# Attention and experts on one core: the first three pairs' steps reordered, a masked low operand, constant rows by one copy

## The chip, the cores and the metric

The kernel runs on one core of a Trainium2 chip. The metric is the device time of one execution in microseconds (us), lower is better. TensorE is called PE, VectorE DVE, ScalarE ACT, GpSimd POOL and SyncE SP, as in the profile.

## What is computed

The reference is attention with pooled queries, and then a mixture of experts on its output.

```python
def _attn_ref(q, k, v):                       # 8 batches, 8 heads, 1152 keys, head size 64
    q_pool = q.reshape(B, H, S // 2, 2, D).mean(axis=3)
    scores = scale * np.matmul(q_pool, k.transpose(0, 1, 3, 2))
    scores = scores - np.max(scores, axis=-1, keepdims=True)
    attn = np.exp(scores)
    attn = attn / (np.sum(attn, axis=-1, keepdims=True) + 1e-09)
    return np.matmul(attn, v)
# moe on x = attn_out as (4608, 512): 8 experts, hidden size 1024
e_idx = np.argmax(x @ w_gate, axis=1)
gate_w = softmax(x @ w_gate)[arange, e_idx];  eom = 1 / (1 + np.exp(-(x @ w_output_gate)))
out[mask] = gate_w[mask, None] * eom[mask, e, None] * (np.maximum(x[mask] @ w1[e], 0) @ w2[e])
```

## The kernel before, in words

The attention part works on 32 pairs of heads (8 batches, 4 pairs each), one after the other, and the expert part follows. To keep float32 accuracy with float16 matmuls, every operand is kept as a high part and a low part, the rest that the high part leaves.

For each pair, `prep` holds a set of small steps. The keys (`kpf`) and the summed queries (`qs`) are scaled by a power of two that comes from the magnitude of the keys (`kabs` on ACT, a matmul `gk`, three tiny DVE steps `ksc`), then split into high parts (`xk`, `xq`) and low parts (`kp`, `yq`). From these come the operands of the matmuls: `ka` (high keys, twice), `kb` (low keys in rows 0 to 63 and constant rows 64 to 68), `qa` (high and low queries), `qb` (high queries and rows for the row maxima), and `qd` (a block of high queries for the low keys of the mixed tile, in which 64 queries of the first head and 64 of the second share a tile). Pairs 3 and later get these operands by DMA copies. The first pair gets them by matmuls with selection matrices (`sk` for the high keys, `sl` for the low keys, `sq0` and `sq1` for the queries, each by key half or head) and casts out of PSUM. The second pair gets its high keys that way and the rest by DMA. The values are split in the same manner (`amax`, `gmax`, `scale`, `vh`, `vs`, `vl`).

Then three generators run, interleaved by hand:

- `mgen` makes the row maxima. A pair has 9 query tiles with 3 key chunks each, so 27 maxima: two matmuls (three for the mixed tile) into one of three PSUM banks, and one DVE reduction (line 397). After a group of 5 and a group of 4 tiles the maxima are combined (line 404), turned by a PE transpose (line 431), split in two pieces `mr` (lines 435 and 436) and sent into `qb` by two DMAs in ACT's queue (line 146).
- `sgen` makes the scores (line 474), 18 a pair, each 128 keys by 512 queries in two matmuls; the second one, with `qb`, takes the maximum off, so the first score waits for the DMAs of the first group. ACT takes the exponential (line 450). The low part of the result is made by POOL (line 458), or for some scores by DVE (line 455) from a second exponential that ACT writes (line 452). The scores have four PSUM banks.
- `agen` multiplies with the values (lines 503 to 505), six scores behind.

The order on PE, DVE, ACT and POOL is what the program writes. The main loop makes one score per step `s` and asks `prep_at` three times a step (one "row" each) for the steps of the tables that are due: `PREPF` for the first pair, `PREP0` for the second, `PREPE` for the third, `PREP` for the others. A table entry is a row number and a step. `L0` says how many steps before the first score the maxima begin, and `LS` by how much that lead grows per step. `WARM` says how many dummy matmuls on a constant (`idle`, line 129) stand at some places; the first number is that of the dummies at the program's very start.

At the start, DVE fills rows of `qb`, POOL builds the identity, the constants and the selection matrices, and three POOL fills (line 199) write the constant rows 64 to 68 of the first `kb`, 2304 columns of float16 each: first all five rows, then four, then three over them. Copies of these rows go to the other two `kb` by DMA.

Of the kernel before, what the change touches and what calls it, by code (L numbers as in the profile page):

```python
# [17 lines left out]
PSUM = bass.MemoryType.PSUM  # L18

LEAD = 18  # L20
L0 = 15
LS = 0.2
RI = 7
PREP0 = ((0, 'lk'), (6, 'qsum'), (8, 'kabs'), (11, 'gk'), (12, 'ksc', 0), (12, 'ksc', 1), (13, 'ksc', 2), (14, 'ks', 0), (15, 'kh', 0), (15, 'qs'), (16, 'ks', 1), (17, 'kh', 1), (18, 'qh'), (18, 'kl'), (19, 'ql'), (19, 'dq', 0), (20, 'dq', 1), (22, 'qd'), (23, 'sk', 0, 0), (26, 'sk', 0, 1), (29, 'sk', 1, 0), (32, 'sk', 1, 1), (28, 'dkl', 0), (28, 'dql', 0), (29, 'dkl', 1), (29, 'dql', 1),
        (53, 'lv'), (71, 'amax', 0), (74, 'amax', 1), (81, 'gmax'), (82, 'scale', 0), (85, 'scale', 1), (90, 'scale', 2), (93, 'vh', 0), (93, 'vs', 0), (96, 'vh', 1), (97, 'vl', 0), (100, 'vs', 1), (104, 'vl', 1))
PREPF = ((0, 'lf'), (1, 'fsel'), (2, 'qsv', 0), (3, 'kabs'), (3, 'gk'), (3, 'ksc', 0), (3, 'ksc', 1), (3, 'ksc', 2), (4, 'qsv', 1), (4, 'khs', 0), (5, 'khs', 1), (6, 'klh', 0), (7, 'klh', 1), (8, 'sk', 0, 0), (9, 'sq0'), (10, 'sk', 0, 1), (11, 'sl', 0, 0), (13, 'qd'),
         (45, 'sl', 0, 1), (46, 'sk', 1, 0), (48, 'sk', 1, 1), (51, 'sq1'), (54, 'sl', 1, 0), (57, 'sl', 1, 1), (56, 'lv'),
         (78, 'amax', 0), (82, 'amax', 1), (99, 'gmax'), (100, 'scale', 0), (100, 'scale', 1), (100, 'scale', 2), (103, 'vh', 0), (103, 'vs', 0), (106, 'vh', 1), (107, 'vl', 0), (109, 'vs', 1), (113, 'vl', 1))
FWD = 15
# [45 lines left out]
def attention(tc, qT, kT, vL, wg, keep, xs, cum, pairs, setup, scat, init, exps, moe):  # L75
    nc = tc.nc
    nb = len(pairs) // 4
    with ExitStack() as ctx:
# [1391 lines left out]
```

## Time and profile before

| | us |
|---|---|
| runs | 1398.0, 1397.2, 1404.05 (median 1398.0) |
| profiled execution | 1396.84 |
| its span | 1395.1 |
| PE busy in the span | 1350.2 (97%) |
| DVE busy | 1104.5 (79%) |
| ACT busy | 1033.2 (74%) |
| POOL busy | 968.9 (69%) |
| mean granted PE clock | 0.989 of full |

The span runs from the first to the last instruction of the profiled execution; its own time is 1.74 us longer. Busy time is that of executing instructions. A row of the timeline has the start, the duration, the engine and line, the operation, output and inputs with their shapes, the count of merged instructions, and in brackets the idle time of the engine before it and what ended it. The granted clock is 1.00 at 2.4 GHz and 0.50 at 1.2 GHz.

### The profile page before, as it was taken

How to read it: one execution, taken by the hardware profiler on the slowest of the kernel's cores; microseconds unless marked ns; L12 is line 12 of the kernel's file. 1: busy time of each engine (PE TensorE's matmuls, PEld its weight loads, DVE VectorE, ACT ScalarE, POOL GpSimd, SP SyncE). 2: the span in 40 equal slices, each digit the busy share in tenths (PEclk: the TensorE clock that was granted, in tenths of full speed). 3: DMA queues.
4: the chain of work that ended last, by engine and by line, in shares of the span. 5: the costliest groups of instructions: out<-in, count | busy, mean ns of one | idle time of the engine just before them, and what ended most of it. 6: DMA issues, size and time to landing. Idle time of an engine off the chain costs nothing.

```text
span 1395.1 us, 41903 instructions
## 1 busy us (share of the span) xinstructions
PE 1350.2 (97%) x16827; PEld 935.0 (67%) x16827; DVE 1104.5 (79%) x2615; ACT 1033.2 (74%) x1858; POOL 968.9 (69%) x998
## 2 busy tenths in 40 slices
PE   7899999999999999999999999989999999999998
PEld 4566666766767676766676666666666767767665
DVE  6677886788788888888788788857988787887883
ACT  6788887888988888888888777684557556475672
POOL 6888998999989999999999899874122221322321
PEclk8999999999999999999999999999999999999999
DMA  5345664556547655655565434167876766547762
GB/s 191 105 137 154 179 184 140 155 172 186 168 141 213 175 154 174 179 179 161 169 181 172 126 94 131 50 243 286 309 266 216 271 228 239 198 154 269 269 242 76
DMA packets 103291, 255.76 MB, mean 183 GB/s; under 512 B 13661, under 2 KB 25565, under 8 KB 103087
## 3 DMA queue, kind: packets, MB, share of 16 engines
q1 hardware_dynamic: 92014, 222.55, 50.5%
q0 software_dynamic: 9632, 29.71, 5.9%
q8 instruction: 133, 2.18, 0.7%
q10 hardware_dynamic: 1440, 0.74, 0.2%
q14 instruction: 72, 0.58, 0.1%
HBM read 197.47 MB, written 20.75 MB: 156 GB/s over the span
## 4 chain that ended last, share of the span: by engine, by line
PE 82%; DVE 6%; ACT 4%; DMA 3%; issue 2%; POOL 2%; SPq 0%; ACTq 0%; POOLq 0%; DVEq 0%
PE mp L396 17%; PE sps L474 16%; PE hps L1111 13%; PE av L504 5%; PE av L503 4%; PE av L505 4%; PE yp L1157 4%; PE yp L1156 4%; PE yp L1155 4%; PE sps L484 2%; PE av L514 2%; PE yp L1153 1%; DMA xs<-xb,posi 1%; PE tp L589 1%; PE xps L1092 1%
## 5 line engine op out<-in xcount | busy, mean ns | idle before, releaser
L397 DVE TENSOR_REDUCE pm<-mp 128x1 f32<-128x384 f32 x864 | 449.6, 551 | 109.6 <-PE mp L396 89.7
L458 POOL TENSOR_TENSOR pl<-p 128x512 f16<-128x512 f32 x414 | 425.2, 1044 | 54.0 <-ACT p L450 50.3
L450 ACT ACTIVATE p<-sps 128x512 f32<-128x512 f32 x576 | 340.2, 599 | 123.6 <-PE sps L474 76.8
L396 PE MATMUL mp<-ka,qa 128*128 128x384 f16 x840 | 269.0, 327 | 5.3 <-DVE xl L579 1.7
L505 PE MATMUL av<-vt,pl 128*128 128x65 f16 x2304 | 253.1, 193 | 3.3 <-POOL pl L458 3.1
L503 PE MATMUL av<-vt,p 128*128 128x65 f16 x2304 | 254.0, 193 | 1.4 <-DVE xb L524 1.3
L504 PE MATMUL av<-vt,p 128*128 128x64 f16 x2304 | 253.4, 194 | 0.0
L396 PE MATMUL mp<-kb,qb 66*128 66x384 f16 x768 | 251.6, 328 | 0.0
L503 PEld LDWEIGHTS <-p 128*128 128x128 bf16 x2304 | 215.6, 97 | 32.6 <-DVE xb L524 3.1
L504 PEld LDWEIGHTS <-p 128*128 128x128 bf16 x2304 | 213.8, 98 | 28.5 <-issue 0.2
L474 PE MATMUL sps<-qa,ka 128*128 128x512 f16 x576 | 219.7, 381 | 3.5 <-DVE pl L455 2.4
L474 PE MATMUL sps<-qb,kb 69*128 69x512 f16 x576 | 220.1, 382 | 0.9 <-DMA qb<-mr 0.9
L505 PEld LDWEIGHTS <-pl 128*128 128x128 f16 x2304 | 212.9, 98 | 3.8 <-POOL pl L458 3.4
L1111 PE MATMUL hps<-x,w1h 128*128 128x256 f16 (+2 forms) x1408 | 208.0, 261 | 3.4 <-DVE x L1095 2.0
L1111 PE MATMUL hps<-x,w1l 128*128 128x256 f16 (+2 forms) x704 | 179.1, 261 | 0.0
L1162 POOL DMA_INDIRECT out_dram<-y,ids x35 | 42.4, 1211 | 150.8 <-DVE ids L958 51.5
L1111 PEld LDWEIGHTS <-w1h 128*128 128x128 f16 x1408 | 132.1, 98 | 18.9 <-issue 3.3
L396 PEld LDWEIGHTS <-qa 128*128 128x128 f16 x840 | 82.8, 99 | 74.6 <-issue 4.4
L455 DVE TENSOR_TENSOR pl<-sps,p 128x512 f16<-128x512 f32 x162 | 111.1, 686 | 22.2 <-ACT sps L452 19.4
L396 PEld LDWEIGHTS <-qb 66*128 66x128 f16 x768 | 75.3, 98 | 69.9 <-issue 8.1
L860 POOL DMA_INDIRECT xg<-xs,riD x28 | 39.4, 1408 | 103.8 <-ACT x L1094 77.3
L1157 PE MATMUL yp<-w2h,hl 128*128 128x512 f16 x272 | 103.2, 379 | 4.8 <-DVE hl L1126 4.5
(337 smaller groups left out, 3117.7 us busy)
## 6 DMA issues: line engine op xcount, KB each, us to landing
wst<-in_w_dram SPq DMA_DIRECT2D x64, 512.0 KB
raw1b<-in_w_dram SPq DMA_DIRECT2D x24, 1024.0 KB
raw2b<-in_w_dram SPq DMA_DIRECT2D x24, 1024.0 KB
raw1a<-in_w_dram SPq DMA_DIRECT2D x22, 1024.0 KB
raw2a<-in_w_dram SPq DMA_DIRECT2D x22, 1024.0 KB
vp<-in_vL_dram SPq DMA_DIRECT2D x32, 576.0 KB
kpf<-in_kT_dram SPq DMA_DIRECT2D x31, 576.0 KB
qp<-in_qT_dram SPq DMA_DIRECT2D x31, 576.0 KB
```

Source lines behind the costliest of these rows:

```text
L396: nc.tensor.matmul(mp, lhsT=l, rhs=r, start=j == 0, stop=j == len(ops) - 1)
L397: nc.vector.tensor_reduce(out=pm[:, k:k + 1], in_=mp, axis=AX.X, op=ALU.max)
L450: e_ = nc.scalar.activation(out=p32, in_=x, func=AF.Exp, scale=1.0 / 16)
L455: nc.vector.tensor_tensor(out=pl, in0=x, in1=ph, op=ALU.subtract)
L458: nc.gpsimd.tensor_tensor(out=pl, in0=p32, in1=ph, op=ALU.subtract)
L474: nc.tensor.matmul(x, lhsT=l, rhs=r, start=j == 0, stop=j == 1)
L503: nc.tensor.matmul(av_[:, qb, 0:65], lhsT=hi, rhs=vt[:, h, c, 0:65], start=c == 0 and qb == 0, stop=False)
L504: nc.tensor.matmul(av_[:, qb, 0:64], lhsT=hi, rhs=vt[:, h, c, 66:130], start=False, stop=False)
L505: nc.tensor.matmul(av_[:, qb, 0:65], lhsT=lo, rhs=vt[:, h, c, 0:65], start=False, stop=e and qb == 3 and h == 0)
L1111: nc.tensor.matmul(hp[:, f, 0:v], lhsT=W1[l][g][:, c, fs], rhs=d['x'][:, c, o:o + v], start=f + c + i == 0, stop=f + c + i == 6)
L1155: nc.tensor.matmul(yp, lhsT=d['hh'][:, c, z], rhs=W2[0][:, c], start=c == 0, stop=False)
L1157: nc.tensor.matmul(yp, lhsT=d['hl'][:, c, z], rhs=W2[0][:, c], start=False, stop=c == 7)
```

## The change

The change has these parts.

1. The tables of the first three pairs get other row numbers. In the first pair (`PREPF`), the selections of the first head's first key half come first; those of the second half (`sk 0 1`, `sl 0 1`), of the second head and the second half of the low keys move behind. In the second pair (`PREP0`) the selections and the query steps come later, and all value steps but the load (`lv`) 9 to 12 rows later. In the third pair (`PREPE`) `qs`, `qh`, `dq`, `ql` and `qd` come 6 to 7 rows later, and the DMA copies of the low parts are reordered.
2. `L0` goes from 15 to 13: the maxima begin two steps closer to the first score.
3. The first pair's groups are 4 and 5 tiles instead of 5 and 4, and in the first group the maxima go by key chunk: all four tiles of the first chunk first.
4. `WARM` has 64 instead of 48 dummies at the start, and 22 more behind the first pair's `gk`.
5. The constant rows of `kb` are written to a small tile `kc` of two columns, and one POOL copy spreads it over the 2304 columns, as 1152 float32 words.
6. `qd` is written in full by a POOL scaling with a mask (`hm`, one column per head) in place of two copies of 64 by 64, and needs no fill at the start.

```diff
-L0 = 15
+L0 = 13
...
-PREP0 = ((0, 'lk'), (6, 'qsum'), (8, 'kabs'), (11, 'gk'), ...
+PREP0 = ((0, 'lk'), (6, 'qsum'), (17, 'kabs'), (25, 'gk'), ...
...
-WARM = (48, 30, 32, 0, 12)
+WARM = (64, 30, 32, 0, 12, 22)
...
-        for i in range(2):
-            nc.gpsimd.memset(QDs[i], 0.0)
+        hm = keep['hm']
...
+                kc = sm.tile([KROW, 2], F16, name="kc", bufs=1)
                 for o, w in ((KROW, 16.0 * SHIFT), (68, -1.0), (67, -MLT)):
-                    nc.gpsimd.memset(KBs[0][64:o], w)
+                    nc.gpsimd.memset(kc[64:o], w)
+                nc.gpsimd.tensor_copy(out=KBs[0].bitcast(F32)[64:KROW].rearrange("p h n -> p (h n)"), in_=kc.bitcast(F32)[64:KROW].broadcast_to([KROW - 64, S]))
...
                 nc.tensor.matmul(g[:, 0:1], lhsT=blk, rhs=ak.bitcast(BF16)[:, 1:2], start=True, stop=True)
+                if not n:
+                    idle(ps_a.tile([128, 512], F32, name="idle5", tag="av"), WARM[5])
...
                 for h in range(2):
-                    z = slice(64 * h, 64 * h + 64)
-                    nc.gpsimd.tensor_copy(out=QDs[n % 2][z, z], in_=xq[z, 512 if h == 0 else 0:][:, 0:64])
+                    nc.gpsimd.tensor_scalar(out=QDs[n % 2][:, 64 * h:64 * h + 64], in0=xq[:, 512 if h == 0 else 0:][:, 0:64], scalar1=hm[:, h:h + 1], scalar2=1.0, op0=ALU.mult, op1=ALU.mult)
...
-                for t0, t1 in ((0, 5), (5, 9)):
+                for t0, t1 in ((0, 5), (5, 9)) if n else ((0, 4), (4, 9)):
...
+                    if n == 0 and t0 == 0:
+                        ch.sort(key=lambda x: x[1])
```

DVE, from the first pair's xq to its first reductions. `kp` are the low keys (first half and second half one step each), `sh` is the PSUM output of a selection matmul, `mp` that of a maximum. Before:

```order
L206 TENSOR_SCALAR xq<-qs,ik 128x576
L207 SCALAR_TENSOR_TENSOR yq<-qs,ik,xq 128x576
L215 SCALAR_TENSOR_TENSOR kp_218<-kpf,ik,xk_222 128x576 x2
L270 CAST qa_138<-sh 128x288 x2
L254 CAST kb_132<-sh 64x288 x2
L397 TENSOR_REDUCE pm<-mp_348 128x1
```

The same place on DVE with the change:

```order
L207 TENSOR_SCALAR xq<-qs,ik 128x576
L208 SCALAR_TENSOR_TENSOR yq<-qs,ik,xq 128x576
L216 SCALAR_TENSOR_TENSOR kp_236<-kpf,ik,xk_240 128x576
L273 CAST qa_142<-sh 128x288 x2
L257 CAST kb_136<-sh 64x288 x2
L216 SCALAR_TENSOR_TENSOR kp_236<-kpf,ik,xk_240 128x576
L401 TENSOR_REDUCE pm<-mp_359 128x1
```

The second half of the low keys has moved from ahead of the casts to behind them.

ACT, from the second pair's first scaling to the first exponential. `ka_136` and `ka_140` are the second pair's high keys. With the change (before, the order was that of the steps `qs`, `xq`, the casts mixed with the two sums over `vp`, and then the two DMAs):

```order
L240 ACTIVATE kpf<-kpf,ik 128x576
L286 CAST xk_334<-kpf 128x576
L240 ACTIVATE kpf<-kpf,ik 128x576
L286 CAST xk_334<-kpf 128x576
L257 CAST ka_140<-sh 128x288 x4
L145 DMA qb_145<-mr 1x4x128 x2
L257 CAST ka_140<-sh 128x288 x4
L243 ACTIVATE qs<-qs,ik 128x576
L295 CAST xq<-qs 128x576
L324 ACTIVATE junk,am<-vp 128x576 x2
L454 ACTIVATE p_572<-sps 128x512
```

The DMAs of the row pieces stand ahead of the second four casts, the query steps and the sums.

ACT, from the tenth score of the first pair on: the third pair's steps (`kpf`, `xk`, `qs`, `xq`) and the second pair's sums over `vp` among the exponentials (`p`, `sps`, `pt`). Before:

```order
L450 ACTIVATE p_755<-sps 128x512
L452 ACTIVATE sps<-sps 128x512
L322 ACTIVATE junk,am<-vp 128x576
L283 CAST xk_511<-kpf 128x576
L240 ACTIVATE qs<-qs,ik 128x576
L450 ACTIVATE p_779<-sps 128x512
L452 ACTIVATE sps<-sps 128x512
L450 ACTIVATE pt<-sps 128x384
L322 ACTIVATE junk,am<-vp 128x576
L292 CAST xq<-qs 128x576
L450 ACTIVATE p_835<-sps 128x512
L452 ACTIVATE sps<-sps 128x512
```

The same place on ACT with the change:

```order
L454 ACTIVATE p_786<-sps 128x512
L456 ACTIVATE sps<-sps 128x512
L286 CAST xk_540<-kpf 128x576
L454 ACTIVATE p_806<-sps 128x512
L456 ACTIVATE sps<-sps 128x512
L454 ACTIVATE pt<-sps 128x384
L454 ACTIVATE p_853<-sps 128x512
L456 ACTIVATE sps<-sps 128x512
L454 ACTIVATE pt<-sps 128x384
L243 ACTIVATE qs<-qs,ik 128x576
L454 ACTIVATE p_894<-sps 128x512
L295 CAST xq<-qs 128x576
```

Both sums, `qs` and `xq` have moved behind the exponentials of the eleventh and twelfth scores.

## Rows read from the trace of the kernel before

**Rows 1.** Busy time by stretch: stretch, length, each engine's busy us, clock, DMA.
```profile
0.00:31.00 31.00, 21.09 (x131) 12.71 (x131) 20.42 (x44) 19.46 (x46) 19.82 (x56) 0.83 0.64 209
...
47.40:60.00 12.60, 9.27 (x81) 5.49 (x78) 7.26 (x19) 6.99 (x15) 7.22 (x9) 0.73 0.60 147
...
230.00:500.00 270.00, 268.99 (x4077) 187.44 (x4078) 219.06 (x572) 231.76 (x455) 256.64 (x264) 1.00 0.57 167
```

**Rows 2.** Timeline of the start: start, duration, engine, line, operation, count.
```profile
1.13 4.09 PE L129 MATMUL idle<-ones 128*128 128x128 bf16 x48 [1.13 <-DVE ones L809]
...
4.95 0.81 POOL L196 CAST sel<-ident 128x64 f16<-128x64 f32 x1
...
5.81 6.35 POOL L199 MEMSET kb<- 5x2304 f16 x3
...
8.25 1.96 DVE L206 TENSOR_SCALAR xq<-qs,ik 128x576 f16<-128x576 f32 x1
...
10.24 0.82 DVE L207 SCALAR_TENSOR_TENSOR yq<-qs,ik,xq 128x576 f16<-128x576 f32 x1
...
10.98 1.54 DVE L215 SCALAR_TENSOR_TENSOR kp<-kpf,ik,xk 128x576 f16<-128x576 f32 x2
...
13.17 0.80 DVE L254 CAST kb<-sh 64x288 f16<-64x288 f32 x2
...
15.20 1.39 POOL L289 TENSOR_TENSOR qs<-qp 128x576 f32<-128x576 f32 x1
...
17.32 3.12 DVE L397 TENSOR_REDUCE pm<-mp 128x1 f32<-128x384 f32 x6 [3.35 <-PE mp L396]
```

**Rows 3.** The same timeline, ACT from 15 us to the second pair's first scaling.
```profile
15.05 1.28 ACT L254 CAST ka<-sh 128x288 f16<-128x288 f32 x4
...
19.06 1.17 ACT L219 ACTIVATE kjunk<-kpf 128x1152 f16<-128x1152 f32 x1
...
21.22 0.77 ACT L237 ACTIVATE kpf<-kpf,ik 128x576 f32<-128x576 f32 x1 [0.90 <-DVE ik L233]
```

**Rows 4.** Hand-over to the scores: timelines of DVE and PE, and one chain row.
```profile
26.80 0.17 DVE L404 TENSOR_REDUCE m<-pm 128x5 f32<-128x15 f32 x1
...
27.65 0.27 DVE L436 SCALAR_TENSOR_TENSOR mr<-mr,tp 5x128 f16<-5x128 f16 x1
...
31.06 0.39 PE L474 MATMUL sps<-qb,kb 69*128 69x512 f16 x1 [0.91 <-DMA qb<-mr]
...
31.45 0.66 PE mp L396 x4
```

**Rows 5.** Busy time by stretch, two single microseconds; the clock is third from last.
```profile
7.00:8.00 1.00, 0.16 (x1) 0.10 (x1) 0.19 (x2) 0.52 (x2) 0.94 (x2) 0.59 0.85 217
...
51.00:52.00 1.00, 0.00 (x0) 0.00 (x0) 1.00 (x2) 0.83 (x2) 0.57 (x1) 0.78 0.51 124
```

**Rows 6.** Timelines of ACT, DVE and PE in the hole behind 47 us.
```profile
46.58 0.78 ACT L240 ACTIVATE qs<-qs,ik 128x576 f32<-128x576 f32 x1
...
47.74 0.59 ACT L452 ACTIVATE sps<-sps 128x512 f32<-128x512 f32 x1
...
48.63 0.68 ACT L322 ACTIVATE junk<-vp 128x576 f16<-128x576 f32 x1
...
49.29 0.67 ACT L292 CAST xq<-qs 128x576 f16<-128x576 f32 x1
...
48.36 0.69 DVE L455 TENSOR_TENSOR pl<-sps,p 128x512 f16<-128x512 f32 x1 [1.27 <-ACT sps L452]
...
49.11 0.38 PE L474 MATMUL sps<-qa,ka 128*128 128x512 f16 x1 [1.59 <-DVE pl L455]
...
52.18 0.38 PE L431 MATMUL tp<-ident,m 128*5 128x128 f32 x1 [1.74 <-DVE pm L397]
```

**Rows 7.** POOL: the steps of lines 300 and 347, min/median/max ns, first and last start.
```profile
L300 POOL COPY qd<-xq x64: 226/234/388, 12.2 to 867.0; 64x64 f16<-64x64 f16 x64
...
L347 POOL TENSOR_SCALAR vp<-vp,sc x64: 737/748/764, 35.3 to 912.4; 128x576 f32<-128x576 f32 x64
```

More of the change, by code (lines that the diff above doesn't have):

```diff
@@ L20 @@
 LEAD = 18
-L0 = 15
+L0 = 13
 LS = 0.2
 RI = 7
-PREP0 = ((0, 'lk'), (6, 'qsum'), (8, 'kabs'), (11, 'gk'), (12, 'ksc', 0), (12, 'ksc', 1), (13, 'ksc', 2), (14, 'ks', 0), (15, 'kh', 0), (15, 'qs'), (16, 'ks', 1), (17, 'kh', 1), (18, 'qh'), (18, 'kl'), (19, 'ql'), (19, 'dq', 0), (20, 'dq', 1), (22, 'qd'), (23, 'sk', 0, 0), (26, 'sk', 0, 1), (29, 'sk', 1, 0), (32, 'sk', 1, 1), (28, 'dkl', 0), (28, 'dql', 0), (29, 'dkl', 1), (29, 'dql', 1),
-        (53, 'lv'), (71, 'amax', 0), (74, 'amax', 1), (81, 'gmax'), (82, 'scale', 0), (85, 'scale', 1), (90, 'scale', 2), (93, 'vh', 0), (93, 'vs', 0), (96, 'vh', 1), (97, 'vl', 0), (100, 'vs', 1), (104, 'vl', 1))
@@ L26 @@
-PREPF = ((0, 'lf'), (1, 'fsel'), (2, 'qsv', 0), (3, 'kabs'), (3, 'gk'), (3, 'ksc', 0), (3, 'ksc', 1), (3, 'ksc', 2), (4, 'qsv', 1), (4, 'khs', 0), (5, 'khs', 1), (6, 'klh', 0), (7, 'klh', 1), (8, 'sk', 0, 0), (9, 'sq0'), (10, 'sk', 0, 1), (11, 'sl', 0, 0), (13, 'qd'),
-         (45, 'sl', 0, 1), (46, 'sk', 1, 0), (48, 'sk', 1, 1), (51, 'sq1'), (54, 'sl', 1, 0), (57, 'sl', 1, 1), (56, 'lv'),
-         (78, 'amax', 0), (82, 'amax', 1), (99, 'gmax'), (100, 'scale', 0), (100, 'scale', 1), (100, 'scale', 2), (103, 'vh', 0), (103, 'vs', 0), (106, 'vh', 1), (107, 'vl', 0), (109, 'vs', 1), (113, 'vl', 1))
+PREP0 = ((0, 'lk'), (6, 'qsum'), (17, 'kabs'), (25, 'gk'), (25, 'ksc', 0), (25, 'ksc', 1), (25, 'ksc', 2), (26, 'ks', 0), (26, 'kh', 0), (27, 'ks', 1), (27, 'kh', 1), (29, 'kl'), (32, 'sk', 0, 0), (34, 'sk', 0, 1), (35, 'sk', 1, 0), (36, 'sk', 1, 1), (36, 'qs'), (36, 'qh'), (36, 'ql'), (36, 'dq', 0), (36, 'dq', 1), (36, 'qd'), (36, 'dkl', 0), (36, 'dql', 0), (36, 'dkl', 1), (36, 'dql', 1),
+        (53, 'lv'), (83, 'amax', 0), (86, 'amax', 1), (93, 'gmax'), (94, 'scale', 0), (97, 'scale', 1), (100, 'scale', 2), (102, 'vh', 0), (102, 'vs', 0), (105, 'vh', 1), (106, 'vl', 0), (109, 'vs', 1), (113, 'vl', 1))
@@ new lines @@
+PREPF = ((0, 'lf'), (1, 'fsel'), (2, 'qsv', 0), (3, 'kabs'), (3, 'gk'), (3, 'ksc', 0), (3, 'ksc', 1), (3, 'ksc', 2), (4, 'qsv', 1), (4, 'khs', 0), (5, 'khs', 1), (6, 'klh', 0), (8, 'sk', 0, 0), (9, 'sq0'), (10, 'sl', 0, 0), (11, 'klh', 1), (13, 'qd'),
+         (56, 'lv'), (60, 'sk', 0, 1), (62, 'sl', 0, 1), (63, 'sk', 1, 0), (66, 'sk', 1, 1), (67, 'sq1'), (69, 'sl', 1, 0), (72, 'sl', 1, 1),
+         (89, 'amax', 0), (91, 'amax', 1), (102, 'gmax'), (102, 'scale', 0), (102, 'scale', 1), (103, 'scale', 2), (104, 'vh', 0), (104, 'vs', 0), (106, 'vh', 1), (107, 'vl', 0), (109, 'vs', 1), (113, 'vl', 1))
@@ L29 @@
 FWD = 15
 PREP = ((8, 'lk'), (11, 'qsum'), (15, 'kabs'), (23, 'gk'), (23, 'ksc', 0), (23, 'ksc', 1), (24, 'ksc', 2), (24, 'ks', 0), (24, 'ks', 1), (24, 'qs'), (28, 'kh', 1), (32, 'qh'), (35, 'qd'), (39, 'kh', 0), (40, 'kl'), (41, 'dk', 0), (45, 'ql'), (50, 'dq', 1), (53, 'dk', 1), (54, 'dkl', 0), (54, 'dql', 0), (56, 'dkl', 1), (58, 'dq', 0), (63, 'dql', 1)) + tuple((r + FWD, *x) for r, *x in ((77, 'lv'), (88, 'amax', 0), (92, 'amax', 1), (99, 'gmax'), (100, 'scale', 0), (100, 'scale', 1), (105, 'scale', 2), (105, 'vh', 0), (109, 'vh', 1), (110, 'vs', 0), (110, 'vl', 0), (110, 'vs', 1), (111, 'vl', 1)))
-PREPE = ((6, 'lk'), (18, 'qsum'), (20, 'kabs'), (26, 'gk'), (27, 'ksc', 0), (28, 'ksc', 1), (29, 'ksc', 2), (31, 'ks', 0), (32, 'ks', 1), (33, 'kh', 0), (35, 'kh', 1), (35, 'kl'), (35, 'qs'), (36, 'dk', 0), (37, 'dk', 1), (37, 'qh'), (39, 'dq', 0), (40, 'dq', 1), (40, 'ql'), (43, 'qd'), (44, 'dkl', 0), (44, 'dql', 0), (46, 'dkl', 1), (46, 'dql', 1)) + ((78, 'lv'), (97, 'amax', 0), (103, 'amax', 1), (108, 'gmax'), (109, 'scale', 0), (110, 'scale', 1), (114, 'scale', 2), (115, 'vh', 0), (116, 'vs', 0), (118, 'vl', 0), (122, 'vh', 1), (122, 'vs', 1), (125, 'vl', 1))
+PREPE = ((6, 'lk'), (18, 'qsum'), (20, 'kabs'), (26, 'gk'), (27, 'ksc', 0), (28, 'ksc', 1), (29, 'ksc', 2), (31, 'ks', 0), (32, 'ks', 1), (33, 'kh', 0), (35, 'kh', 1), (35, 'kl'), (36, 'dk', 0), (37, 'dk', 1), (41, 'qs'), (43, 'qh'), (46, 'dq', 0), (47, 'dq', 1), (47, 'ql'), (50, 'qd'), (44, 'dkl', 0), (46, 'dkl', 1), (51, 'dql', 0), (53, 'dql', 1)) + ((78, 'lv'), (97, 'amax', 0), (103, 'amax', 1), (108, 'gmax'), (109, 'scale', 0), (110, 'scale', 1), (114, 'scale', 2), (115, 'vh', 0), (116, 'vs', 0), (118, 'vl', 0), (122, 'vh', 1), (122, 'vs', 1), (125, 'vl', 1))
@@ L818, in keep_tiles @@
         nc.gpsimd.memset(half[:, h, 64 * h:64 * h + 64], 1.0)
+    hm = t('hm', [128, 2], F32)
+    nc.gpsimd.memset(hm, 0.0)
+    for h in range(2):
+        nc.gpsimd.memset(hm[64 * h:64 * h + 64, h:h + 1], 1.0)
     nc.gpsimd.iota(t('em8', [128, 5, 8], F32), pattern=[[0, 5], [1, 8]], base=-8, channel_multiplier=0, allow_small_or_imprecise_dtypes=True)
```

## Prediction

> **What bounds it.** I read the busy time by stretch first. From 230 to 500 us TensorE (PE) is busy 268.99 of 270 us at the full clock: nothing that this change touches can be gained there. The missing time is early: 21.09 busy of 31 us at the start, and 9.27 of 12.6 us from 47.4 on, at a mean clock of 0.73 [rows 1]. So I follow two stretches: the one up to the first score, and the hole behind 47.4 us. The timeline of the start shows what its pieces wait for [rows 2, 3], the hand-over to the scores is in [rows 4], the clock's falls in [rows 5], the hole in [rows 6], POOL's prices in [rows 7].
>
> At the start a row of VectorE (DVE) steps leads: xq, yq, the low keys, the casts, and at 17.32 the first of the reductions that make the row maxima [rows 2]. The first score's second half waits for those maxima to come back by DMA, at 31.06 [rows 4]. In the hole PE waits twice, 1.59 and 1.74 us [rows 6]. The first time a DVE step of line 455 stands in the way, which waits 1.27 for ScalarE (ACT); the second time it is reductions that stand in DVE's queue behind the next step of that line. ACT is late because it is full of preparation: qs, the |V| sums, xq.
>
> **Term 1, constant rows.** Three POOL fills take 6.35 us from 5.81 on, about 2.1 each; the second ends near 10.0 [rows 2]. xq on DVE starts at 8.25 inside it, takes 1.96 and ends 0.2 behind it, at 10.21. Steps of the same width take 0.82 (yq) and 0.77 (half of 1.54), and a cast of half its width 0.4 [rows 2]. I take 0.6 for xq without the fill: 1.35 us less (1.1 to 1.6; nothing if 1.96 is its own price). The copy that replaces the fills has 1152 columns; POOL's nearest step needs 0.748 for 576 [rows 7], so 1.5, at most the 2.1 of a fill: from about 6.0 to 7.5 or 8.1, over before 8.25.
>
> The Trainium skill ("SBUF — State Buffer", Who interferes with whom) says that DVE and GpSimd share a port pair as an exclusive lock, which certain DVE copies and scalings take, and that a DVE step with two SBUF inputs also fights a GpSimd step that reads SBUF. The trace bears both out: xq above, and the POOL cast of line 196, which took 0.81 for 64 columns where the scaling of 576 takes 0.748 [rows 2, 7]. By it there is a price as well: POOL's addition qsum, which reads, now runs beside the second half of the low keys and could hold it for its own 1.39 us [rows 2]. My sum leaves that out; by the page it would be up to 1.4 smaller, an estimate.
>
> **Term 2, up to the first reduction.** With xq from 8.25 to 8.85, yq ends at 9.6, the low keys' first half at 10.35, two qa casts at 11.15, two kb casts (0.80 in rows 2) at 11.95. The second half of the low keys now stands behind the kb casts and ends at 12.7. The shifts of the second half and the second head stand behind PE's first maximum now, so that waits for kb alone: 12.0. DVE's first reduction comes at 12.7 instead of 17.32, 4.6 us earlier.
>
> **Term 3, up to the first score.** The first group has 12 maxima instead of 15. DVE alone needs 0.52 each (3.12 for six, rows 2), 6.2 us. But ACT is slower: 14 casts of 0.32 from 12.4 on (1.28 for four) put the second pair's magnitude at 16.9. It takes 1.17, and the scale is there 0.99 later (20.23 to 21.22), at 19.1; the last three maxima stand behind it on PE and DVE, 3 x 0.52: 20.7 [rows 2, 3]. From there to the finished row pieces took 1.12 (26.80 to 27.92, rows 4), and 0.1 of DVE before it: 21.9. The DMA commands stand in ACT's queue behind two scalings (0.77 each), two casts (0.67, rows 6) and four small casts, 2.9 + 1.28 from 19.1 on: the last starts near 23.0. From the pieces to the score took 3.14 (27.92 to 31.06): 26.2. If ACT's queue runs ahead, 25.0; if each shift waits, 27.5. I take 26.2, the middle: 4.9 us earlier. Only 19 maxima stand ahead of this score instead of 22; the three left cost PE 0.33 each later (0.66 for two, rows 4), 1.0. **Net 3.9 us** (2.5 to 5).
>
> The 38 added dummies cost nothing that I can see: at 85 ns each (4.09 for 48, rows 2) the first 64 end at 6.6, before the one matmul that PE has between 7 and 8 us [rows 5], and the 22 behind that take 1.9, to some 9.6. Until then PE waits for xq and yq anyway; the first key shift may come 0.5 later, and its casts have until 11.15.
>
> **Term 4, the hole.** Ahead of the second exponentials of the eleventh and twelfth scores the new order takes off ACT one |V| sum (0.68) and qs (0.78), then another |V| sum and xq (0.67) [rows 6]. About 0.1 of each lies under the step before it, so that is 1.3 and 2.4 us. The first wait, 1.59, shrinks to 0.3, the second, 1.74, goes. Then PE doesn't stop long enough for the clock to fall at 51.6 [rows 5]. A mean of 0.73 over 12.6 us is 6.8 us at half speed, of which PE worked 6.2: 3.1 us more. Together 1.3 + 1.74 + 3.1 = **6.1 us** (bounds 0 and the whole 6.4). The moved pieces come later in the same stretch, where ACT rests: 6.99 busy of 12.6 [rows 1].
>
> **Term 5, given back.** What was moved now has less time. The third pair's q steps come some seven rows later, the second pair's value steps nine to twelve rows later (three rows are a score), and POOL, which the hole had given rest (7.22 busy of 12.6, rows 1), gets the same work in less time. I reckon one or two waits of a microsecond: **2 us** (0 to 6.4, the hole's whole price).
>
> **Term 6, the masked low operand.** Two POOL steps of 64 columns a pair in place of two of 0.234 [rows 7]. A scaling of 576 columns takes 0.748, so 64 take 0.15 to 0.75. POOL is busy 256.64 of 270 us [rows 1], and a pair takes 27.8 us (the two scalings a pair run from 35.3 to 912.4, 64 of them, rows 7), so 1.38 us a pair is free: nothing, even at 0.75 (1.03 more).
>
> **Sum.** 3.9 + 6.1 - 2 = 8.0 us. The profiled execution took 1396.84 (span 1395.1): 1388.8. The median of the runs shown, 1398.0, is 1.2 above it, so I forecast **1390.0 us** for the median; 1386 to 1393 in this case. About 0.5%, 7 us here, is what a measurement can tell from no change, so the line is at 1391.0.
>
> **Rivals.** *The clock falls in the start.* PE gets its work in drips between 8 and 20 us. Before, the clock fell at 7.2 after PE had stopped at 5.2 [rows 2, 5]. Two maxima then take PE about 1.3 instead of 0.66, more than DVE's 1.04; for the 19 maxima and the shifts that is up to 3 us: 1393. For it: the gaps of term 3. Against: the dummies, which bridge the gap in which it fell. The Trainium skill ("TensorE: Matmul & The Clock Gate", Part 1) has half speed as the default, which activity releases; the fall at 7.2 agrees.
>
> *The hole comes back.* Another late operand (the third pair's rows, the second pair's values behind a POOL without rest) takes the place of line 455, and the clock falls again. Then only the start's gain stays: 1398.0 - 3.9 = 1394, to 1397 if the start is poor too. For it: POOL's rest in the hole goes, and everything that it does there has to fit in less time. Against: the moved work of ACT is some 3 us, and it rests 5.6 us there.
>
> *Slower: the masked step is dear.* If a two-operation scaling of 64 columns costs POOL over 0.234 + (1.38 + 0.25)/2 = 1.05 us, POOL becomes the bound in all 32 pairs and eats the 8 us; at 1.2 us it is 1.93 - 1.38 = 0.55 a pair, 17.6 in all, 1407.6. Against: 576 columns take 0.748 today.
>
> **How the numbers follow.** Forecast 0.62, clock 0.14, hole back 0.20, dear step 0.04. Of the first, about 0.84 lies under 1391.0, of the clock case a quarter: faster 0.56; slower 0.04; within 0.5% the rest, 0.40. The range runs from 1386.0, all gains and little given back, to 1396.0, which takes in the clock case and most of the hole's.
>
> **What would show it.** Right: xq under 0.8 us; first reduction near 12.7; first score's second half near 26; no wait of PE over 1 us and no clock under 1.0 from there to 55 us; a masked step under 0.4 us. Wrong: xq still near 2 us; clock 0.5 after 10 us; PE waiting for the second pair's low rows at its first maximum, or for the second pair's V behind POOL; or the lead of the first 60 us gone by 230.

## The result and the profile after

The changed kernel takes **1382.1 us** (median of 6 runs, 1381.5 to 1385.05) against 1397.6 (6 runs, 1395.5 to 1404.05): a ratio of 0.989, 95% interval 0.987 to 0.991. Forecast were 1390.0 us and 1386 to 1396: the direction is right, the gain is twice as large, and the time lies below the range. The profiled execution took 1383.9 us, its span 1382.1 (1395.1 before).

First the stretches of [rows 1], in the changed kernel (columns as there), with one more behind the hole:

```profile
0.00:31.00 31.00, 24.20 (x191) 15.84 (x191) 21.46 (x51) 22.14 (x51) 18.42 (x60) 1.00 0.62 211
47.40:60.00 12.60, 12.60 (x172) 8.46 (x171) 9.57 (x26) 9.46 (x20) 11.57 (x14) 1.00 0.72 230
72.00:76.00 4.00, 4.00 (x46) 2.69 (x44) 2.61 (x6) 3.21 (x8) 2.57 (x5) 0.57 0.74 208
230.00:500.00 270.00, 269.26 (x4104) 188.38 (x4101) 221.95 (x578) 234.95 (x466) 255.55 (x263) 1.00 0.58 171
```

The hole is closed: PE works 12.60 of 12.6 us where it worked 9.27, at a clock of 1.00 where it was 0.73. The clock doesn't fall in the start either. But there is a new stretch at a clock of 0.57, from 72 to 76.

The timeline of the start (DVE, then POOL), beside [rows 2]:

```profile
8.30 0.50 DVE L207 TENSOR_SCALAR xq<-qs,ik 128x576 f16<-128x576 f32 x1
...
11.83 0.80 DVE L216 SCALAR_TENSOR_TENSOR kp<-kpf,ik,xk 128x576 f16<-128x576 f32 x1
12.55 0.54 DVE L401 TENSOR_REDUCE pm<-mp 128x1 f32<-128x384 f32 x1
```
```profile
6.27 1.14 POOL L200 COPY kb<-kc 5x1152 f32<-5x1152 f32 x1
8.99 1.64 POOL L302 TENSOR_SCALAR qd<-xq,hm 128x64 f16<-128x64 f16 x2 [1.58 <-DVE xq L207]
...
11.15 0.86 POOL L547 CAST wgt<-wf 128x64 fp32r<-128x64 f32 x1
12.10 0.71 POOL L548 TENSOR_TENSOR wgt<-wf,wgt 128x64 fp32r<-128x64 f32 x1
```

xq takes 0.50 instead of 1.96, the first reduction comes at 12.55 instead of 17.32. The hand-over, beside [rows 4] (PE, then ACT):

```profile
25.61 0.39 PE L478 MATMUL sps<-qb,kb 69*128 69x512 f16 x1
```
```profile
24.36 1.31 ACT L257 CAST ka<-sh 128x288 f16<-128x288 f32 x4 [1.28 <-PE mp L400]
25.52 0.81 ACT L243 ACTIVATE qs<-qs,ik 128x576 f32<-128x576 f32 x1
26.36 0.67 ACT L295 CAST xq<-qs 128x576 f16<-128x576 f32 x1
26.94 0.68 ACT L324 ACTIVATE junk<-vp 128x576 f16<-128x576 f32 x1
...
27.74 0.68 ACT L324 ACTIVATE junk<-vp 128x576 f16<-128x576 f32 x1
...
28.42 1.06 ACT L454 ACTIVATE p<-sps 128x512 f32<-128x512 f32 x2
```

The first score is finished 5.45 us earlier, but its exponential starts only 3.1 us earlier (28.42 against 31.5): the second pair's query steps and sums now stand ahead of it on ACT.

**Where the time comes from.** For each of the 576 exponentials of line 450 (454 after) and those of the tails one can subtract its start after from its start before. This lead grows in steps, so each step can be followed to its place. In the table each column is one exponential, named by its start in the kernel before; each row is one profiled execution, the e rows are the experiments below. The median is that of all runs, and "gain" is how far it lies under the median of the kernel before that ran beside it. These medians of the kernel before differ by up to 2.8 us from group to group, so runs of different groups are compared by their gain or their lead, and not by the bare median.

| kernel | median us | gain | 31.5 | 42.0 | 61.8 | 86.2 | 205 | 237 | 442 | 706 | 842 | 931 |
|---|---|---|---|---|---|---|---|---|---|---|---|---|
| changed | 1382.1 | 15.5 | 3.1 | 4.2 | 9.0 | 6.5 | 6.1 | 10.4 | 10.1 | 11.9 | 14.7 | 14.8 |
| e1 mask alone | 1389.2 | 8.1 | -0.8 | -0.8 | 0.6 | 0.6 | 1.4 | 5.7 | 2.2 | 2.2 | 5.6 | 5.8 |
| e2 without mask | 1394.4 | 2.9 | 3.1 | 4.1 | 9.0 | 6.6 | 6.6 | 10.9 | 9.7 | 4.5 | 3.2 | 3.4 |
| e3 three fills | 1385.4 | 11.9 | -0.7 | 0.4 | 5.2 | 4.3 | 4.4 | 8.3 | 8.9 | 10.5 | 13.6 | 13.7 |
| e4 few dummies | 1382.4 | 14.9 | 1.4 | 2.5 | 7.3 | 6.4 | 6.4 | 10.7 | 11.4 | 13.0 | 15.7 | 15.8 |
| e5 half mask | 1389.3 | 9.6 | 3.1 | 4.3 | 9.1 | 6.8 | 6.3 | 10.7 | 11.7 | 13.0 | 5.9 | 6.1 |
| e6 old tables 2, 3 | 1391.6 | 7.4 | -0.2 | -0.4 | 1.6 | -2.8 | -2.8 | 1.5 | 2.8 | 4.3 | 7.2 | 7.3 |
| e7 old table 3 | 1385.9 | 13.0 | 3.4 | 4.4 | 8.5 | 3.7 | 3.9 | 8.2 | 7.8 | 9.1 | 12.0 | 12.1 |
| e8 weights later | 1380.2 | 18.8 | 3.0 | 4.1 | 9.0 | 9.4 | 8.8 | 13.1 | 14.7 | 16.0 | 18.6 | 18.7 |
| e9 half mask, PSUM | 1380.8 | 19.2 | 2.9 | 4.1 | 8.9 | 8.0 | 8.1 | 12.2 | 13.2 | 14.2 | 17.2 | 17.2 |
| e10 before, half mask | 1399.3 | 0.7 | 0.0 | 0.0 | 0.1 | 0.1 | 0.0 | 4.4 | 5.2 | 6.7 | -0.8 | -0.8 |
| e11 e8, few dummies | 1382.4 | 17.6 | 1.3 | 2.4 | 7.2 | 7.6 | 8.4 | 12.6 | 12.6 | 14.6 | 16.0 | 16.0 |
| e12 old qd, later | 1384.9 | 15.1 | 2.9 | 3.9 | 8.7 | 6.3 | 6.3 | 10.1 | 11.3 | 10.2 | 12.4 | 12.5 |
| e13 e10, PSUM | 1389.6 | 10.5 | 1.3 | 1.3 | 2.7 | 1.2 | 2.1 | 6.5 | 6.3 | 7.0 | 10.3 | 10.4 |
| e14 old first pair | 1387.7 | 12.4 | 0.5 | -3.5 | 1.3 | -0.5 | -0.8 | 3.5 | 3.9 | 4.6 | 7.8 | 7.9 |
| e15 e8, PSUM | 1382.5 | 17.6 | 3.2 | 4.3 | 9.1 | 9.5 | 9.1 | 13.3 | 14.0 | 15.6 | 18.2 | 18.3 |

The part that I had argued about, the first 205 us, gives 6.1. From 205 to 237 us come another 4.3, and from 706 to 842 another 2.8, in stretches of which the prediction has no word. In the kernel before, POOL and PE show this there (POOL's timeline at two places, PE's, the chain of waits, the stretches):

```profile
219.06 1.00 POOL L683 DMA_INDIRECT xs<-xb,posi  x1 [0.17 <-issue]
220.08 3.04 POOL L458 TENSOR_TENSOR pl<-p 128x512 f16<-128x512 f32 x3
223.06 0.24 POOL L300 COPY qd<-xq 64x64 f16<-64x64 f16 x1
227.86 0.23 POOL L300 COPY qd<-xq 64x64 f16<-64x64 f16 x1 [4.56 <-DMA xs<-xb,posi]
...
786.55 0.23 POOL L300 COPY qd<-xq 64x64 f16<-64x64 f16 x1 [3.45 <-DMA xs<-xb,posi]
```
```profile
229.26 0.23 PE L505 MATMUL av<-vt,pl 128*128 128x65 f16 x1 [2.71 <-POOL pl L458]
```
```profile
219.06 8.65 DMA xs<-xb,posi
```
```profile
222.00:224.00 2.00, 2.00 (x34) 1.57 (x33) 1.98 (x6) 2.00 (x6) 1.30 (x3) 1.00 1.01 317
...
228.00:230.00 2.00, 0.73 (x11) 0.74 (x12) 0.00 (x0) 0.00 (x0) 1.92 (x3) 0.76 0.02 6
230.00:232.00 2.00, 2.00 (x7) 0.91 (x8) 1.15 (x4) 0.40 (x1) 2.00 (x2) 0.50 0.00 1
```

The first of the two `qd` copies runs at once. The second stands 4.56 us, until the router's scatter DMA (`xs<-xb,posi`, rows of the attention output to memory), issued by POOL 4 us earlier, has landed after 8.65. Behind the copy wait POOL's low parts, for them PE, 2.71 us, and then PE's clock is 0.50 from 229.0 to 232.5, another 1.7: together 4.4, about the 4.3. Behind the wait of 3.45 us PE stops four times between 787 and 807 us, for 0.43, 0.89, 0.31 and 1.03 us; the changed kernel has no stop over 0.28 there. That is about the 2.8. The data of the copy have nothing to do with that DMA. The wait stands in the instruction stream, on the copy of the second head, whose block begins at partition 64:

```
L300 COPY qd_143<-xq 64x64
L300 COPY qd_143<-xq 64x64 [waits DMASW2_49,DMASW3_49,DMASW1_49,DMASW4_49,DMASW0_49,Pool_49]
```

DMASW are the semaphores of POOL's DMAs, Pool that of its own instructions. In the trace (waits ahead of the `qd` step, before and with the change):

```profile
L300 POOLq EVENT_SEMAPHORE  x19: 17/43/6221, 216.8 to 808.9; - x19
```
```profile
L302 POOLq EVENT_SEMAPHORE  x1: 17/17/17, 8.8 to 8.8; - x1
```

The 19 stand at seven places, all with semaphores of the scatter DMAs. A copy of that form has the wait on its own engine in each pair from the second on, and at these seven places the scatter DMAs with it. Written to partitions 0 to 63, or to all 128, it has neither behind the first pair. Why it gets them only there, no run here shows. In the changed kernel the masked step, on all partitions, runs through (POOL's timeline):

```profile
212.98 0.99 POOL L687 DMA_INDIRECT xs<-xb,posi  x1 [0.17 <-issue]
213.98 3.05 POOL L462 TENSOR_TENSOR pl<-p 128x512 f16<-128x512 f32 x3
217.00 0.61 POOL L302 TENSOR_SCALAR qd<-xq,hm 128x64 f16<-128x64 f16 x2
217.58 1.03 POOL L462 TENSOR_TENSOR pl<-p 128x512 f16<-128x512 f32 x1
```

### The profile page after: what moved, and what is told of

It reads as the page before. It is cut to its first block, busy times and chain, and to the rows that moved or that the text cites. A ratio compares the mean times of both kernels' runs of the same rounds, so it can differ in the third digit from the quotient of the medians.

```text
span 1382.1 us, 41951 instructions
## 1 busy us (share of the span) xinstructions
PE 1347.6 (98%) x16865; PEld 934.1 (68%) x16865; DVE 1101.0 (80%) x2615; ACT 1031.7 (75%) x1858; POOL 970.6 (70%) x1000
## 5 line engine op out<-in xcount | busy, mean ns | idle before, releaser
L459 DVE TENSOR_TENSOR pl<-sps,p 128x512 f16<-128x512 f32 x162 | 111.1, 686 | 21.7 <-ACT sps L456 18.2
```

Of the source, the lines that this page charges most:

```text
L459: nc.vector.tensor_tensor(out=pl, in0=x, in1=ph, op=ALU.subtract)
```

## Experiments

Theory: the change took away a wait that I had not priced. Rival: the reordering made the whole gain, and the late steps of the lead are its echo. The kernel before was run beside each group of experiments, with medians of 1397.3 (e1 to e4), 1399.0 (e5 to e8), 1400.0 (e9 to e12) and 1400.1 us (e13 to e15).

### The mask alone, and all but the mask

e1, to the kernel before:
```diff
-                    nc.gpsimd.tensor_copy(out=QDs[n % 2][z, z], in_=xq[z, 512 if h == 0 else 0:][:, 0:64])
+                    nc.gpsimd.tensor_scalar(out=QDs[n % 2][:, 64 * h:64 * h + 64], in0=xq[:, 512 if h == 0 else 0:][:, 0:64], scalar1=hm[:, h:h + 1], scalar2=1.0, op0=ALU.mult, op1=ALU.mult)
```


> The kernel before with one part of the change alone: the masked layout of qd (mask, two scalings of 64 columns a pair, no fill). Theory (a wait that I priced at nothing): before the change, the second qd copy of a pair stood on POOL until the router's scatter DMAs had landed, 4.56 us at 223 to 228 us and 3.45 us near 783 to 787 us; the masked step has no such wait. In the traces the lead of the changed kernel grows by 4.3 us around 205 to 237 us and by some 4 us from 700 to 842 us, so this part alone should give about 8: 1389.5 us, 1387 to 1392, and no idle time over 1 us before the masked step on POOL. Rival (the reordered start alone made the time, and the later gain is work that merely shifted): no change, 1396 to 1399. My prediction's own figure for this part was nothing.

1389.2 us, ratio 0.994 (0.992 to 0.996): 8.1 us, as the theory said. No idle time over 0.3 us is left on POOL ahead of `qd`. The lead of the profiled execution (1392.0 us) grows at the two places, by 4.3 and 3.4. Between them it loses 3.5: PE waits 1.86 us at 426.2 for a DMA of row pieces, a stop that the kernel before doesn't have, and its clock falls (PE's timeline):

```profile
428.04 0.39 PE L472 MATMUL sps<-qb,kb 69*128 69x512 f16 x1 [1.86 <-DMA qb<-mr]
```

e2 is the changed kernel with the reverse of that diff.

> The changed kernel with the old qd: two fills at the start and two copies of 64 by 64 a pair. Theory of the wait: the lead at 60 to 200 us stays (6.1 us), the POOL wait of 3 to 5 us returns near 217 and again near 775 us, PE stops behind the first one and its clock falls to 0.5, and the time is 1382.1 + 8 = 1390 us (1388 to 1392). That would be the time that I had forecast for the whole change. Rival (reordering alone shifts the scatter DMAs away from the copy): 1382 to 1384 and no such wait.

1394.4 us, ratio 0.998 (0.996 to 1.000): without the mask, 12.3 of the 15.5 us are gone. The rival falls, but my figure of 1390 was too low, and so was the place: the waits are 1.19 us at 218 and 1.28 at 329, and then (POOL's timeline)

```profile
546.89 0.99 POOL L689 DMA_INDIRECT xs<-xb,posi  x1 [0.16 <-issue]
...
556.26 0.23 POOL L304 COPY qd<-xq 64x64 f16<-64x64 f16 x1 [5.15 <-DMA xs<-xb,posi]
...
669.27 0.23 POOL L304 COPY qd<-xq 64x64 f16<-64x64 f16 x1 [3.18 <-issue]
```

The lead is the changed kernel's up to 321 us (11.2), then falls: by 4.4 between 442 and 571, where the first of these waits is, by 0.8 from there to 706, where the second is, and by 1.3 between 706 and 842, where PE waits 1.88 us for a DMA at 760.9 and its clock falls. The changed kernel gains 4.6 from 442 to 842. So the reordering only made the wait near 218 short; the later ones, and the stop at 760.9, took most of its lead back. Without the mask all the rest of the change is worth 2.9 us.

### The wait without the layout

e12 leaves the old copies and moves the step by two scores: in `PREP`, `(35, 'qd')` becomes `(41, 'qd')`.

> The changed kernel with the old qd, and this step 6 rows (two scores, some 3 us) later in pairs 3 to 31. Without the mask the copy stood 4.0 us behind the last scatter DMA's issue (547 against 551 us) and waited up to 5.15 us there and 3.18 us near 666; now it stands some 7 us behind. Theory (the price of the wait is what is left of the scatter's landing when POOL reaches the copy): waits of at most 2.2 us instead of 5.15, most of them gone, 1382 to 1387 instead of 1394.4, without any mask. Rival (the copies cost by their shape or number): 1393 to 1396.

1384.9 us, ratio 0.988 (0.986 to 0.990): 9.4 us less than e2, with the old copies. At 553.30 both stand 7.3 us behind the DMA's issue, and neither waits over 0.13 us (POOL's timeline):

```profile
545.97 1.00 POOL L689 DMA_INDIRECT xs<-xb,posi  x1 [0.17 <-issue]
...
553.30 0.60 POOL L304 COPY qd<-xq 64x64 f16<-64x64 f16 x2
```

The price is what is left of the DMA's flight. The median lies 2.8 us above the changed kernel's, but the gain, 15.1, is nearly its 15.5; the lead at 931 us is 2.3 smaller, and for that I can name no single cause.

e5 masks the second head's half alone, in the changed kernel; the first head's is a copy to partitions 0 to 63, and the two fills at the start are back.
```diff
-                for h in range(2):
-                    nc.gpsimd.tensor_scalar(out=QDs[n % 2][:, 64 * h:64 * h + 64], in0=xq[:, 512 if h == 0 else 0:][:, 0:64], scalar1=hm[:, h:h + 1], scalar2=1.0, op0=ALU.mult, op1=ALU.mult)
+                nc.gpsimd.tensor_copy(out=QDs[n % 2][0:64, 0:64], in_=xq[0:64, 512:576])
+                nc.gpsimd.tensor_scalar(out=QDs[n % 2][:, 64:128], in0=xq[:, 0:64], scalar1=hm[:, 1:2], scalar2=1.0, op0=ALU.mult, op1=ALU.mult)
```


> The changed kernel with the mask on the second head's half alone: the first head's half is again a copy of 64 by 64 at partitions 0 to 63 (with the fills at the start). Without the mask the changed kernel took 1394.4 us, and the wait for the scatter DMAs stood only on the copy at partitions 64 to 127. Theory (it is that one copy's wait, not the layout or the duration of the step): no wait over 1 us before qd on POOL and 1382 us (1380.5 to 1384). Rival (two small copies as such are what POOL stumbles over, or the dropped fills): 1386 to 1394.

1389.3 us: by the number a miss. But `qd` doesn't wait, and up to 706 us the lead is 13.0, above the changed kernel's. Then 7.1 us go at one place (DVE's timeline, then POOL's):

```profile
766.49 0.15 DVE L893 COPY mx<-tp 128x1 f32<-128x1 f32 x1
766.67 7.56 DVE L894 TENSOR_TENSOR tp<-cn,mx 128x8 f32<-128x8 f32 x1
774.14 1.01 DVE L403 TENSOR_REDUCE pm<-mp 128x1 f32<-128x384 f32 x2
```
```profile
766.34 1.00 POOL L689 DMA_INDIRECT xs<-xb,posi  x1 [0.17 <-DMA qb<-xq]
767.36 3.04 POOL L464 TENSOR_TENSOR pl<-p 128x512 f16<-128x512 f32 x3
770.33 0.24 POOL L303 COPY qd<-xq 64x64 f16<-64x64 f16 x1
...
771.84 2.35 POOL L291 TENSOR_TENSOR kp<-kpf,xk 128x1152 f16<-128x1152 f32 x1
778.21 0.83 POOL L464 TENSOR_TENSOR plt<-pt 128x384 f16<-128x384 f32 x1 [4.02 <-ACT pt L456]
```

A comparison of 8 columns, part of the choice of the first expert, takes 7.56 us (0.18 in the changed kernel) and ends when POOL's unbroken row of steps ends, at 774.2. PE stops 7.63 us. e10, the same half mask on the kernel before, fell into the same pit:

> The kernel before with the half mask alone (first head's half a 64 by 64 copy at partitions 0 to 63, second head's half a masked scaling of 128 by 64). Theory of the wait: no wait over 1 us at qd, so as the whole mask alone gave: 1389 us (1387 to 1392). Rival (the layout matters beyond the wait): 1394 or more.

1399.3 us; no wait at `qd`, a lead of 6.7 us at 706, then the comparison takes 7.52 us at 772.6. In e9 (from e5) and e13 (from e10) it reads the maximum from PSUM, so that one of its two SBUF inputs goes:
```diff
-        V.tensor_copy(out=ms, in_=mx)
-        V.tensor_tensor(out=eq, in0=cn, in1=ms.broadcast_to([128, 8]), op=ALU.is_equal)
+        V.tensor_tensor(out=eq, in0=cn, in1=mx.broadcast_to([128, 8]), op=ALU.is_equal)
```


> The half mask of the experiment before, with one DVE step changed: the comparison that took 7.56 us at 766.7 us for 8 columns (0.17 us in the changed kernel) reads the maximum from PSUM and no longer a copy of it in SBUF, so it has one SBUF input instead of two. POOL worked without a break from 767.36 to 774.2 us, and DVE's next step began at 774.14. Theory (the two-input step stands against POOL's stream of reading steps; it comes free when POOL pauses): the stop of PE from 767.1 to 774.7 us and the 5.1 us of clock loss behind it... together a lead of 7.1 us by the exponentials, are gone: 1382.2 us (1380.5 to 1383.5). Rival (something else held DVE, and the half mask is worse by itself): 1388 to 1390.

> The kernel before with the half mask, and the comparison of 8 columns reading the maximum from PSUM. Theory (the half mask took away the wait, and the 7.52 us of the two-input step at 772.6 us took its gain back): 1399.3 - 7.5 to 8 = 1391 to 1392, at most 2 us above the whole mask's 1389.2, no such stop at 773 us. Rival (the half mask gains nothing on the kernel before): 1396 to 1400.

1380.8 us, and 1389.6, ratio 0.992 (0.990 to 0.995). (The 5.1 us of clock loss in the expectation count the stop too: of the 10.2 us at a clock of 0.50, from 770.9 to 781.1, PE worked 6.3, so it is 3.2.) In e9 (DVE's timeline):

```profile
765.21 0.16 DVE L892 TENSOR_TENSOR tp<-cn,tp 128x8 f32<-128x8 f32 x1
```

So the half mask, once the comparison doesn't stop it, moves the kernel before by 10.5 us, the whole mask by 8.1, with intervals that overlap: it is the one wait, not the layout. The PSUM edit alone was not run on the kernel before; the comparison stands there once and takes 0.17 us, so it has no such stop to take away. The edit also takes a copy of 0.15 us away ahead of the comparison, which therefore starts earlier; that the second input alone did it is not shown.

### The start

e3 writes the constant rows by three fills again, in the changed kernel.

> The changed kernel with the constant rows by three POOL fills again. Prediction's term 1: xq takes about 1.96 instead of 0.50 us, the first reduction comes about 1.4 us later than 12.55, near 14, and the second half of the constant rows holds the first maximum no longer than that; time 1383.5 us (1382.5 to 1385). Rival (the fills cost more, since the three fills end near 12.2 us and the selection casts and the query sum queue behind them on POOL): first exponential 3 us later than 28.4, 1385 to 1386. Rival (1.96 is xq's own price): no change, 1382.

1385.4 us, 3.3 more: the first rival. xq takes 1.79 and the first reduction comes at 13.89, as I had said, but the first score's second half only at 29.15 instead of 25.61. 1.3 us late at the first reduction grew to 3.5.

e4 takes the 38 dummies away.

> The changed kernel with 48 dummies at the start and none behind the first gk. My prediction: the dummies are what keeps PE's clock from falling at 7 us, where it fell before the change; without them the clock is 0.5 from about 7 to past 10 us, and later drips may let it fall again. If the maxima up to the first score run at half speed in part, the first exponential comes 1 to 3 us later than 28.4: 1383 to 1385. Rival (DVE and ACT set the pace of the start, PE only follows): the clock falls and nothing else moves, 1382.

1382.4 us: nothing. Yet the clock is 0.50 from 9.8 to 16.7 us and the first exponential 1.7 us later. Between 62 and 86 us the changed kernel loses 2.5 of its lead, e4 only 0.9: PE waits 1.74 us at 69.3 for a cast on ACT, and then the clock is 0.50 from 72.6 to 76.0. e4 has the same wait (1.75) and no fall. e8 takes that wait away: the sums over the expert weights (`WS0`, 18 to 30) no longer stand on ACT ahead of the cast.

> The changed kernel with the sums over the expert weights beginning 12 scores later, so that the first of them no longer stands on ACT at 67.0 us, ahead of the cast that PE waits 1.74 us for at 69.3 us; behind that wait PE's clock falls at 72.6 us and 1.7 us go. Theory: the wait shrinks to 0.6 us or less and the clock doesn't fall there: 1 + 1.7 = 2.7 us less, 1379.4 (1378.5 to 1380.5). Rival (the fall just moves to the next gap, or the sums crowd the later scores): 1381 to 1383.

1380.2 us (1379.6 to 1386.0). PE's timeline, the changed kernel and then e8:

```profile
71.05 0.32 PE L400 MATMUL mp<-ka,qa 128*128 128x384 f16 x1 [1.74 <-DVE xl L583]
```
```profile
69.72 0.32 PE L400 MATMUL mp<-ka,qa 128*128 128x384 f16 x1 [0.71 <-DVE xl L583]
```

No fall follows there, and the lead at 86 us is 9.4 instead of 6.5. e11 is e8 with few dummies:

> The sums over the expert weights 12 scores later (1380.2 us with the change's dummies), and 48 dummies at the start and none behind the first gk. With few dummies the first exponential came 1.7 us later, but the changed kernel lost 1.7 us to a clock fall at 72.6 us that the other did not have, so both took 1382. Theory (the dummies are worth 1.7 us, and were paid back by that fall alone): without the fall they differ by it: 1381.9 us (1381 to 1383.5). Rival (the dummies are worth nothing, what is won is lost elsewhere): 1380 to 1380.8.

1382.4 us (1381.5 to 1382.5): 2.2 more than e8, the theory's number. The lead does not bear the theory out. Without the dummies the first exponential is 1.7 us behind e8's, but at 205 us only 0.4 is left of it: e8 loses 0.6 at 109 us, where PE waits 1.52 us, and e11 has no such wait. Between 237 and 442 us the distance grows by 1.6 again, far from the dummies. So they bring the first exponential 1.7 us forward, in e4 and here; that they are worth anything at the end is not shown, and the number was luck.

### The tables of the first three pairs

e6 has the second and third pairs' tables of the kernel before, e7 the third's alone, e14 the first pair's table, `L0` and groups.

> The changed kernel with the second and third pairs' tables of the kernel before. Prediction's term 4: the hole behind the first ten scores comes back, two waits of some 1.6 and 1.7 us and a clock fall of 1.7 to 3.4 us: the lead at the 17th exponential shrinks from 9.7 us by 4 to 6, and of it 2 come back later because the fall near 72 us goes: 1385 to 1387. And the second pair's old early steps stand in ACT's and DVE's queues ahead of the first maxima: first exponential 1 to 3 us later. Rival (the hole is closed by the earlier start alone): within 1 us of 1382.

> The changed kernel with only the third pair's table of the kernel before. If the third pair's query scaling and its cast are what makes ACT late in the hole (in the trace of before they stand directly ahead of the late exponentials), the second wait there comes back in part, 1 to 1.7 us, perhaps with a clock fall of 1.7: 1382 to 1385. Rival (the second pair's value sums alone did it): same as the changed kernel, 1381 to 1383.

> The changed kernel with the first pair's table, L0 and groups of the kernel before (15 maxima in the first group, in the order of tiles). Prediction's term 3: 15 maxima instead of 12 before the first score and DVE's first reduction behind the whole of the low keys: the first exponential 2 to 4 us later than 28.4, of which 1 comes back: 1384 to 1386. Rival (the gain of the start came from the short xq and the second pair's later steps alone): 1381 to 1383.

1391.6, 1385.9 and 1387.7 us, each above what I expected. By the gain they lose 8.1, 2.5 and 3.1 of the change's 15.5 us, and only e6 is clearly beyond the expectation. PE's waits behind it:

e6:
```profile
31.24 0.39 PE L478 MATMUL sps<-qb,kb 69*128 69x512 f16 x1 [1.91 <-DMA qb<-mr]
...
49.47 0.38 PE L478 MATMUL sps<-qa,ka 128*128 128x512 f16 x1 [1.50 <-DVE pl L459]
```
e7:
```profile
56.05 0.39 PE L478 MATMUL sps<-qb,kb 69*128 69x512 f16 x1 [2.40 <-DMA qb<-mr]
```
e14:
```profile
35.71 0.50 PE L398 MATMUL mp<-ka,qa 128*128 128x384 f16 x1 [2.78 <-DMA qa<-yq]
```

e6 brings back the first wait of the hole and loses the start. In e7 and e14 it is not ACT that is late, but a DMA: a row order that fits ACT can still put a transfer too late. Behind e6's stop at 62.9 (3.14 us, for a DMA of row pieces too) and behind e7's the clock falls, 1.7 us each; in e14 it is 0.50 from 34.6 to 41.5 us.

Last, e15 puts the PSUM comparison on e8:

> The changed kernel with the weight sums 12 scores later and the comparison reading from PSUM. If the two stalls are apart: the comparison took only 0.17 us in the changed kernel, so nothing from it here, and the time is that of the later weight sums, 1380.2 us (1378 to 1381), with no clock fall between 30 and 900 us. Rival (phases shift and another fall comes in its place): 1381 to 1384.

1382.5 us (1380.8 to 1388.05): no clock fall between 30 and 900 us, a lead of 18.3 at 931 as e8 has, but three falls in the expert part behind 920 us. Its runs and e8's overlap, so I read no difference. e8 and e9 beat both kernels by their medians. Against the changed kernel, 3.3 and 3.7 us of gain, the intervals of the ratios overlap (0.987 to 0.991 there, 0.986 to 0.991 and 0.984 to 0.988 here), so that they are faster than it is not shown.

## Why the prediction was right and wrong

- **Terms 1 and 2** held: xq 0.50 (0.6), the copy 1.14 (1.5), first reduction 12.55 (12.7). The price that I left out of the sum did not come: the low keys' second half took 0.80 us. The Trainium skill ("SBUF — State Buffer", Who interferes with whom) has that price for a DVE step with two SBUF inputs beside a GpSimd step that reads. Here POOL's addition qsum came at 13.82, behind it, and it was POOL's small steps that got longer: the addition of 64 columns at 12.10, beside the second half, took 0.71 us where it took 0.32 before, and the cast of 64 columns at 11.15, mostly beside DVE's casts, 0.86 where it took 0.24.
- **Term 3**: the score's second half came at 25.61 (26.2), the first exponential 3.1 earlier; at the ninth exponential the lead is 4.2 where I had 3.9 net. The rows up to the score were right. Behind it I had only the three maxima that come later, 1.0; that ACT holds the first exponential I had not named, so it is in part luck that 4.2 lies so near 3.9. That the dummies cost nothing holds: without them the first exponential comes 1.7 us later (e4, e11). By 205 us nothing of that is left in e4 and 0.4 in e11.
- **Term 4**: no wait of PE over 0.25 us from 40 to 61 us, clock 1.00. The lead grows from 4.2 to 9.0, 4.8 us, where I had 6.1.
- **Term 5**: 2.9 given back (2): 1.7 of it is the clock fall at 72.6.
- Together 6.1 us by 205 us instead of 8.0: inside the bounds. But a lead by 205 us is not yet time: without the mask only 2.9 us of gain come out at the end (e2), so terms 1 to 5, which I had added up as time, hold only where the wait of term 6 is gone too.
- **Term 6 failed.** "Two POOL steps of 64 columns a pair in place of two of 0.234", "nothing". This is the step of the prediction that failed. The steps cost what I said, 0.317 each (0.85 and 0.80 in the first pair, beside DVE's yq and low keys). But I priced their durations and POOL's free time and not the wait of the instruction that goes: 4.56 and 3.45 us on POOL, 2.71 on PE, 1.7 of clock. Taking it away gave 8.1 us alone and 12.3 as the last part. These waits stood in the trace of before, in the idle time ahead of line 300 and in PE's longest wait between 60 and 900 us. I had read PE's stretch from 230 to 500, which begins just behind it, and concluded that nothing could be gained.
- The rivals: the clock did not fall in the start and the hole did not come back. "Slower" was the wrong sign for the masked step. A rival with its wait removed was missing, and the range had no room below.
- Between 442 and 706 us the lead grows by 1.8 that I can give to no single place, and 1.8 of the final 14.8 go in the expert part.

## What to carry to other kernels

When an instruction is replaced, price its waits and not only its duration: read the idle time ahead of its line, and who waits behind it, over the whole run. A wait for a transfer that the data don't need can hide in the shape of a small copy, and costs by phase: two stops in one version, others in the next. And after reordering, ask for each PE stop that is left whether a clock fall follows it; the same 1.74 us cost 1.74 in one version and 3.4 in another.

## What the runs showed of the hardware that I had not expected

- A DVE step of 8 columns with two SBUF inputs took 7.56 and 7.52 us (e5, e10), beside seven POOL steps in a row, of 0.24 to 2.35 us, and ended when POOL paused. The Trainium skill ("SBUF — State Buffer", SBUF: two separate sides) has the shared port pair held for the whole instruction by whichever starts first. If that is what held the step, which these runs don't show, it held it not through one POOL step but through all seven. In the changed kernel the same step, at 767.77, beside the issue of a scatter DMA too, took 0.18; what decides is open.
- A scatter of 128 rows stood 8.65 us between its issue and its landing, in a stretch with the DMA engines full (1.01 of their time at 222 to 224 us).
- After the same wait of PE, 1.74 us, the granted clock fell to 0.50 for 3.4 us in the changed kernel, and did not in e4, e9 and the kernel before.
